# Earlier maxima of w1, q in long rows, and the tangent on one engine, in a fused attention and two-layer-pair kernel

## The chip, the cores and the metric

The kernel runs on one core of a Trainium2 chip. The metric is the device time of one launch in microseconds (us). Of the kernel before there are three timed runs and one profiled execution.

## The reference

What is computed, with the shapes that matter (B = 8 batches, H = 8 heads, S = 576 positions, D = 64; 4608 tokens, 512 model columns, 2048 hidden columns):

```python
kv = einsum('bhsd,bhse->bhde', k, v)
out = einsum('bhsd,bhde->bhse', q, kv)
rms = sqrt(mean(out * out, axis=-1, keepdims=True) + 1e-06)
x = (out / rms * g_norm)            # -> (4608, 512) tokens x columns
h = x @ moe_w_in                    # (512, 2048)
x = maximum(0.01 * h, h) @ moe_w_out    # (2048, 512)
h = x @ moe2_w_in
out = (h - tanh(h)) @ moe2_w_out
```

q, k, v and g_norm come as 32-bit floats, the four weights as 64-bit floats, which the kernel reads as pairs of 32-bit words.

## The kernel before, in words

The work has five stages. First comes a **start** of some 85 us: the attention of batch 0 and most of batch 1, and the making of the first weight matrix. Then come four **phases** of matrix products (one per weight matrix), in which TensorE works on the 16-bit halves of operands.

**Products.** Each phase multiplies by Strassen's method: of every 2x2 block of operands seven products are formed (the loop over `order` in `up`, the tables `PROD` and `BANK_OF`), and each product is three 16-bit matmuls per slice (high times high, high times low, low times high; line 513 in `three`). For that each operand is cut into seven forms: three blocks as they are and four sums. The names in the profile: `opa` holds the three plain forms of a left operand, `ops` the four sums, `w` the weights, `ps_a` to `ps_d` are the accumulators, `c` and `u` partial results kept by ScalarE, `g` the result, added up by VectorE (line 575).

**Weights.** `convert` turns one unit (of 16 per matrix) of 64-bit words into 32-bit floats: ScalarE takes the upper words' absolute values (line 329), VectorE clamps them and takes their maximum along (line 333), shifts, and puts in the lower words and the sign (lines 340, 346, 352). When all 16 units are through, `weight_scale` (lines 265 to 280) makes a scale from the greatest value: a reduction, a small transpose on TensorE (`pt`, line 234), two VectorE operations, a small matmul that spreads it (`pb`, line 244), then `s_w` and for w1 `s1g`. `right_stages` makes the forms of a unit: ScalarE writes the high halves (line 378) and VectorE the low ones (line 381), in two pieces of three and four blocks each, and the sums between (lines 388 and 392) are GpSimd's. The second and third matrix are converted while the first two phases run.

**Attention.** `load_pair` loads k, v and q of two heads (lines 812 and 818), k and v in rows of 1536 bytes, q in pieces of 256 bytes, so that both heads' columns lie side by side. `pair` gives TensorE the steps: `pk` (k times v, line 834, twelve small matmuls at two column positions), `pq` (q turned, line 854, two groups of three transposes of 96 by 128), `po` (line 870), and after every second pair `pm` (the means, line 907). ScalarE copies `kvd` and `qt` (lines 845, 862) and squares (line 876). `norms` takes the root and the reciprocal (lines 929, 937), stores them to HBM, loads them back broadcast as `bc` (lines 940, 946), and GpSimd multiplies `xg` by them (line 952). `left_stages` then makes `opa` and `ops` (lines 452 and 459; the four sums on GpSimd, line 491).

**The tangent.** In phase three `tanh` has ScalarE compute tanh of a whole 128x1024 tile (line 1246); VectorE subtracts one half of it and GpSimd the other (both line 1249).

**Order.** Every engine executes its queue in the order in which it was written. That order comes from a planner (class `Plan`): each step has an estimated duration, `fit` finds a free stretch on its engine, and what is due is issued in order of planned time. TensorE's own sequence is fixed by `on_pe`, at a planned time `plan.pe` that begins at `START`; in `between1` the attention steps of later batches are put between the products. If a step is planned before what it needs, the planner stops with an assertion.

Of the kernel before, what the change touches and what calls it, by code (L numbers as in the profile page):

```python
# [27 lines left out]
PROD = {1: (6, 5), 2: (4, 4), 3: (0, 6), 4: (5, 0), 5: (3, 1), 6: (1, 2), 7: (2, 3)}  # L28
BLOCKS = ("11", "21", "12", "22")
NOP = 7  # L30
# [18 lines left out]
class Plan:  # L49
# [7 lines left out]
    def __init__(self):  # L57
        self.heap, self.n, self.pe = [], 0, 0.0
        self.taken = {e: [] for e in "AVG"}

# [50 lines left out]
    def on_pe(self, dur, fn):  # L111

        self.at(self.pe, fn)
        self.pe += dur
        return self.pe

    def run(self):
        while self.heap:
            self.now, _, fn = heapq.heappop(self.heap)
            fn()  # L120


class Slots:


    def __init__(self, pool, kind, nbytes, n):
        self.pool, self.kind, self.nbytes = pool, kind, nbytes
        self.idle = list(range(n))
# [12 lines left out]
def body(ctx, tc, q, k, v, g_norm, w1, w2, w3, w4, out):  # L141
    nc = tc.nc
    B, H, S, D = q.shape
    NT, DM = out.shape
    DFF = w1.shape[1]
# [12 lines left out]
    const = ctx.enter_context(tc.tile_pool(name="const", bufs=1))  # L158
    wpool = ctx.enter_context(tc.tile_pool(name="wpool", bufs=1))
    work = ctx.enter_context(tc.tile_pool(name="work", bufs=1))  # L160
    dram = ctx.enter_context(tc.tile_pool(name="dram", bufs=1, space=DRAM))
    ps = ctx.enter_context(tc.tile_pool(name="ps", bufs=1, space=PSUM))
    L, M, X = Slots(work, "l", 16 * T1, NL), Slots(work, "m", 2 * 2 * NOP * P, NM), Slots(work, "x", 4 * T1, NX)
    plan = Plan()
# [4 lines left out]
    def bank(n, name):  # L169
        assert n not in used, (n, name)  # L170
        used.add(n)
        return ps.tile([P, 512], F32, tag=f"p{n}", name=name)

# [16 lines left out]

    def need(what):
        assert what in done_, ("planned too late", plan.now, what)
# [12 lines left out]
    sel = const.tile([P, 2 * Q - 2], F32, name="sel")  # L205
    kvd = [const.tile([P, P], F32, name=f"kvd{n}") for n in range(2)]

    def constants():
        for h in range(2):
            nc.sync.dma_start(out=gcol[D * h:D * h + D, :], in_=g_norm.rearrange("(p o) -> p o", o=1))  # L210
        make_identity(nc, ident)
# [3 lines left out]
        for n in range(2):  # L215
            nc.vector.memset(sel[D * n:D * n + D, Q - 2 + n:Q - 1 + n], 1.0 / D)
            nc.vector.memset(kvd[n], 0.0)
        nc.vector.tensor_reduce(out=gabs, in_=gcol, axis=AX.X, op=ALU.max, apply_absolute_value=True)
# [41 lines left out]
    def weight_scale(n, t):  # L260
# [16 lines left out]
        def last():  # L277
# [3 lines left out]
            done_.add(f"s_{name}")  # L281
# [25 lines left out]
    def convert(n, i, kk, t, land, keep=None):  # L307
# [42 lines left out]
        def high():  # L350
# [5 lines left out]
            converted[n] += 1  # L356
            if converted[n] == 2 * NP:
                weight_scale(n, plan.now + 1.0)

        def store():  # L360
            done_.add(("wf", n, i, kk))
            nc.sync.dma_start(out=wf[n, i, kk], in_=held["ap"])
            M.give(held["o"])

        slow = 1.0 if keep else 1.1
        steps = [(None, land, load), (None, 0.0, room), ("A", 0.7, one), ("V", 0.72 * slow, two), ("V", 0.4 * slow, shift),
                 ("V", 0.63 * slow, low), ("V", 0.63 * slow, high)]
        plan.chain(t, steps + ([(None, 0.0, store)] if keep is None else []))

    def right_stages(w, dst, scale, minus4, merged=False):  # L370
# [3 lines left out]
        def cols(n0, n1):  # L374
            return w().rearrange("p (o c) -> p o c", c=P)[:, n0:n1]

        def hi(a, b, n):
            nc.scalar.activation(out=dst()[:, 0, a:b], in_=cols(0, n), func=AF.Identity, scale=scale())  # L378

        def lo(a, b, n):  # L380
            nc.vector.scalar_tensor_tensor(  # L381
                out=dst()[:, 1, a:b], in0=cols(0, n), scalar=scale(), in1=dst()[:, 0, a:b],
                op0=ALU.mult, op1=ALU.subtract,
            )

        def both(e):
            b = w().rearrange("p (o c) -> p o c", c=P)
# [959 lines left out]
```

## Time and profile before

| | |
|---|---|
| Median of 3 runs | 1518.32 us (1515.48 to 1521.1) |
| Profiled execution: time, span | 1515.43 us, 1513.7 us |
| TensorE busy | 1440.1 us (95%) |
| VectorE busy | 1248.8 us (83%) |
| ScalarE busy | 914.5 us (60%) |
| GpSimd busy | 687.4 us (45%) |
| DMA | 323.17 MB in 188926 packets, 54112 of them under 512 B |

The span is the time from the first to the last instruction of the profiled execution; the 1.7 us between it and the time lie around it. PE is TensorE, PEld its weight loads, DVE VectorE, ACT ScalarE, POOL GpSimd, SP the engine that issues the DMAs. "PEclk" is the granted clock of TensorE as a share of full speed. A busy share is a mean over stages, and each stage is to be read by itself. In a timeline, the number in brackets is the idle time of the engine before the row, and behind it is what ended it; consecutive rows overlap at their edges, so the pace of a stream is the distance between starts.

### The profile page before, as it was taken

How to read it: one execution, taken by the hardware profiler on the slowest of the kernel's cores; microseconds unless marked ns; L12 is line 12 of the kernel's file. 1: busy time of each engine (PE TensorE's matmuls, PEld its weight loads, DVE VectorE, ACT ScalarE, POOL GpSimd, SP SyncE). 2: the span in 40 equal slices, each digit the busy share in tenths (PEclk: the TensorE clock that was granted, in tenths of full speed). 3: DMA queues.
4: the chain of work that ended last, by engine and by line, in shares of the span. 5: the costliest groups of instructions: out<-in, count | busy, mean ns of one | idle time of the engine just before them, and what ended most of it. 6: DMA issues, size and time to landing. Idle time of an engine off the chain costs nothing. (4 is left out here: it accounts for less than half of the span.)

```text
span 1513.7 us, 32951 instructions
## 1 busy us (share of the span) xinstructions
PE 1440.1 (95%) x12658; PEld 1192.3 (79%) x12658; DVE 1248.8 (83%) x2019; ACT 914.5 (60%) x1525; POOL 687.4 (45%) x646
## 2 busy tenths in 40 slices
PE   5299999999899999999999999999998999999998
PEld 3167777777677777777777888888887888888887
DVE  4885777787777899999997888978999988888871
ACT  5377777777667645445543677778887554445540
POOL 0474330452542455445442355558885643444430
PEclk8589999999999999999999999999999999999999
DMA  9829998999978845555645866546768644444431
GB/s 265 202 62 249 289 297 247 312 281 328 305 243 283 327 154 186 199 176 176 202 162 189 320 220 211 205 169 223 266 246 300 240 156 144 146 147 141 143 96 36
DMA packets 188926, 323.17 MB, mean 214 GB/s; under 512 B 54112, under 2 KB 130912, under 8 KB 188768
## 3 DMA queue, kind: packets, MB, share of 16 engines
q1 hardware_dynamic: 188768, 321.06, 65.9%
q8 instruction: 99, 1.62, 0.4%
q14 instruction: 59, 0.48, 0.1%
HBM read 190.84 MB, written 130.15 MB: 212 GB/s over the span
## 5 line engine op out<-in xcount | busy, mean ns | idle before, releaser
L513 PEld LDWEIGHTS <-w 128*128 128x128 f16 x8400 | 819.6, 98 | 204.0 <-issue 29.7
L491 POOL TENSOR_TENSOR gl<-gl 128x256 f32<-128x256 f32 (+1 forms) x272 | 297.0, 1094 | 368.9 <-DVE gl L491 142.2
L513 PE MATMUL ps_a<-ops,w 128*128 128x288 f16 (+1 forms) x2400 | 330.9, 282 | 6.7 <-ACT u L564 4.8
L513 PE MATMUL ps_c<-ops,w 128*128 128x288 f16 (+1 forms) x2352 | 315.3, 282 | 12.2 <-DVE g L575 12.2
L513 PE MATMUL ps_a<-opa,w 128*128 128x288 f16 (+1 forms) x2016 | 283.8, 281 | 0.2
L513 PEld LDWEIGHTS <-ops 128*128 128x128 f16 x1728 | 169.1, 98 | 21.6 <-issue 2.0
L513 PE MATMUL ps_b<-opa,w 128*128 128x288 f16 (+1 forms) x1200 | 175.5, 283 | 0.0
L491 DVE TENSOR_TENSOR gl<-gl 128x256 f32<-128x256 f32 (+1 forms) x272 | 151.5, 558 | 4.3
L1249 POOL TENSOR_TENSOR g<-g,th 128x512 f32<-128x512 f32 x72 | 113.3, 1574 | 82.1 <-ACT th L1246 68.8
L513 PEld LDWEIGHTS <-opa 128*128 128x128 f16 x1296 | 126.8, 98 | 14.7
L461 DVE SCALAR_TENSOR_TENSOR ops<-gl,inv,ops 128x1024 f16<-128x1024 f32 x72 | 102.9, 1429 | 29.4 <-ACT ops L454 29.3
L952 POOL TENSOR_TENSOR xg<-xg,bc 128x1152 f32<-128x1152 f32 x16 | 47.4, 2967 | 174.7 <-DMA bc<-iv 125.7
L454 ACT ACTIVATE ops<-gl,inv 128x1024 f16<-128x1024 f32 x72 | 82.4, 1144 | 62.9 <-POOL gl L491 62.9
L452 ACT ACTIVATE ops<-gl 128x1152 f16<-128x1152 f32 x64 | 74.3, 1161 | 74.8 <-POOL gl L491 72.8
L575 DVE SCALAR_TENSOR_TENSOR g<-ps_c,u 128x288 f32<-128x288 f32 x128 | 58.1, 454 | 50.3 <-PE ps_c L513 48.5
L459 DVE TENSOR_TENSOR ops<-gl,ops 128x1152 f16<-128x1152 f32 x64 | 93.5, 1461 | 4.8 <-ACT ops L452 4.7
L513 PE MATMUL ps_c<-w,ops 128*128 128x256 f16 x864 | 97.3, 273 | 0.2 <-DVE osb L575 0.2
L513 PE MATMUL ps_a<-w,ops 128*128 128x256 f16 x864 | 95.8, 273 | 1.4 <-ACT c L566 1.4
L566 ACT ACTIVATE u<-ps_a,up 128x256 f32<-128x256 f32 x144 | 68.1, 473 | 47.1 <-PE ps_a L513 43.4
L378 ACT ACTIVATE wo<-unit,s_w 128x384 f16<-128x384 f32 (+1 forms) x96 | 63.1, 662 | 52.3 <-DVE unit L392 45.5
L491 POOL TENSOR_TENSOR x1g<-x1g 128x256 f32<-128x256 f32 x72 | 65.3, 908 | 49.4 <-DVE opa L461 43.0
L381 DVE SCALAR_TENSOR_TENSOR wo<-unit,s_w,wo 128x384 f16<-128x384 f32 (+1 forms) x96 | 84.8, 891 | 1.6 <-ACT wo L378 1.4
(126 smaller groups left out, 2171.0 us busy)
## 6 DMA issues: line engine op xcount, KB each, us to landing
g<-g SPq DMA_DIRECT2D x64, 576.0 KB, 6.4
gl<-g SPq DMA_DIRECT2D x64, 576.0 KB, 4.7
g<-g SPq DMA_DIRECT2D x72, 512.0 KB, 3.3
gl<-g SPq DMA_DIRECT2D x72, 512.0 KB, 4.4
wd<-wo SPq DMA_DIRECT2D x48, 448.0 KB, 3.3
w<-wd SPq DMA_DIRECT2D x24, 896.0 KB, 7.4
words<-in_moe_w_in_dram SPq DMA_DIRECT2D x64, 256.0 KB, 6.2
words<-in_moe_w_out_dram SPq DMA_DIRECT2D x64, 256.0 KB, 4.8
```

Source lines behind the costliest of these rows:

```text
L378: nc.scalar.activation(out=dst()[:, 0, a:b], in_=cols(0, n), func=AF.Identity, scale=scale())
L381: nc.vector.scalar_tensor_tensor(out=dst()[:, 1, a:b], in0=cols(0, n), scalar=scale(), in1=dst()[:, 0, a:b], op0=ALU.mult, op1=ALU.subtract,)
L452: nc.scalar.activation(out=o, in_=i_, func=AF.Copy)
L454: nc.scalar.activation(out=o, in_=i_, func=AF.Identity, scale=scale())
L459: nc.vector.tensor_tensor(out=o, in0=i_, in1=h, op=ALU.subtract)
L461: nc.vector.scalar_tensor_tensor(out=o, in0=i_, scalar=scale(), in1=h, op0=ALU.mult, op1=ALU.subtract)
L491: lambda: e.tensor_tensor(out=g()[:, o], in0=g()[:, a], in1=g()[:, b], op=op),
L513: nc.tensor.matmul(out=out_, lhsT=a, rhs=c, start=start and m == 0, stop=stop and m == n - 1, skip_group_check=not fresh,)
L566: nc.scalar.activation(out=t, in_=src, func=AF.Identity, scale=self.scale)
L575: nc.vector.scalar_tensor_tensor(out=o, in0=src, scalar=self.minus if sub else self.scale, in1=t, op0=ALU.mult, op1=ALU.add,)
L952: e.tensor_tensor(out=x, in0=x, in1=held[kk].ap[:, n0:n1], op=ALU.mult)
L1249: e.tensor_tensor(out=g()[:, n], in0=g()[:, n], in1=held["t"].ap[:, n], op=ALU.subtract)
```

## The change

The start is arranged anew, the attention's q is loaded and turned in another way, the weights' forms are laid out and cut in another way, and phase three's subtraction moves to one engine. In detail:

- **w1.** Units of blocks 5, 6 and 7 (6 of 16) are not converted when they land: VectorE only takes the maximum of their upper words (`most`, line 465), and the rest of the conversion (`later`) comes after the scale. The first ten are converted as before. The loads of batch 1's pairs are put in front of and behind w1's last units, and three of these pairs' steps run directly after batch 0's.
- **Weights' forms.** The sums (`sums`, lines 496 and 500) come first, and high and low halves of all seven blocks are one instruction each (`parts`, lines 516 and 519; `PROD` numbers the blocks anew for that). For w1's first two blocks GpSimd forms the sums before the scale is known.
- **Batch 0's norm.** The reciprocal is one instruction, its broadcast goes through TensorE (`wide`, line 1096, eight matmuls with a selecting matrix `hot`) instead of HBM, and VectorE multiplies (line 1102) and forms the sums.
- **q.** One DMA of 1536-byte rows per pair instead of two of 256-byte pieces, in all batches. The heads are apart in it, so each group of three transposes becomes six plain matmuls against the identity, at column positions 0 and 64 (line 975).
- **The tangent.** VectorE subtracts both halves (line 1419), and GpSimd none.
- **The planner.** It first runs dry and notes, where a step would come before what it needs, by how much TensorE's planned time has to be put off; that moves the planned times, and no instruction waits by it. `SLOW` goes.

```diff
-            apart = nm != "q"
...
-            for h in range(2):
-                nc.sync.dma_start(out=held[nm].ap[:, :, h], in_=src[b, 2 * c + h].rearrange("(p c) d -> p c d", p=CP))
+            held[nm] = L.take([CP, 2, NC, D], F32, nm)
+            nc.sync.dma_start(
+                out=held[nm].ap.rearrange("p h c d -> p h (c d)"),
+                in_=src[b, 2 * c:2 * c + 2].rearrange("h (p c) d -> p h (c d)", p=CP),
+            )
...
-                nc.tensor.transpose(
-                    qt[r][0][:, CP * a:CP * a + CP], two_heads(held["q"], r * NC // 2 + a), ident[:CP, :CP]
-                )
+                for h in range(2):
+                    nc.tensor.matmul(
+                        out=qt[r][0][D * h:D * h + D, CP * a:CP * a + CP], lhsT=held["q"].ap[:, h, r * NC // 2 + a],
+                        rhs=ident[:CP, :CP], start=True, stop=True, tile_position=(0, D * h), skip_group_check=True,
+                    )
...
+        def most():
+            nc.vector.tensor_reduce(
+                out=mw[:, n, 2 * i + kk:2 * i + kk + 1], in_=held["w"].ap[:, 1::2].bitcast(F32), axis=AX.X, op=ALU.max,
+                apply_absolute_value=True,
+            )
+            count(n)
...
+        if later is not None:
+            plan.chain(t, [(None, land, load), ("V", 0.65, most)])
+            later.append([
+                (None, 0.0, room), ("A", 0.7, one), ("V", 0.42, clamp), ("V", 0.42, shift), ("V", 0.69, low), ("V", 0.69, high),
+            ])
+            return
...
+        def hi():
+            nc.scalar.activation(out=dst()[:, 0], in_=cols(), func=AF.Identity, scale=scale())
+
+        def lo():
+            nc.vector.scalar_tensor_tensor(
+                out=dst()[:, 1], in0=cols(), scalar=scale(), in1=dst()[:, 0], op0=ALU.mult, op1=ALU.subtract,
+            )
+
+        return [("A", 1.15, hi), ("V", 1.25, lo)]
...
+            nc.tensor.matmul(
+                out=held["b", kk, n][:, :T1], lhsT=hot["t"].ap[:, kk, n], rhs=held["iv"], start=True, stop=True,
+            )
...
+            nc.vector.tensor_tensor(out=x, in0=x, in1=held["b", kk, n][:, :T1], op=ALU.mult)
...
-        order += [("w",) + u for u in UNITS[hp:hp + 1]]
-    order += [("w",) + u for u in UNITS[4:]]
+        order += [("w",) + u for u in UNITS[2 * hp:2 * hp + 2]]
+    order += [("w",) + u for u in UNITS[8:14]] + [("a", 1, PAIRS[0])] + [("w",) + u for u in UNITS[14:]]
+    order += [("a", 1, PAIRS[hp]) for hp in range(1, 4)]
...
-    START = last + 45.0
+    last = ta[1, PAIRS[0]][0]
+    for hp in range(EARLY):
+        early_pair(1, PAIRS[hp], last + 0.8, ta[1, PAIRS[hp]][1])
+        last += 6.0
+    START = last + GAP
...
-            [("V", 0.65, lambda: two(nc.vector, slice(0, 2))), ("G", 1.5, lambda: two(nc.gpsimd, slice(2, 4)))],
+            ("V", 0.62, lambda: two(0)), ("V", 0.62, lambda: two(1)),
```

Three places show how the queues move. The first is VectorE's queue in the start, around w1's scale (`m_w` is the greatest value, `opa` the attention's operand, `mw` the units' maxima, `xg` the attention's result). Before:

```order
L352 SCALAR_TENSOR_TENSOR w1f_643<-words,w1f_643 128x512 x2
L459 TENSOR_TENSOR opa<-xg,opa 128x288
L265 TENSOR_REDUCE m_w_690<-mw 128x1
L267 TENSOR_SCALAR t_w_691<-m_w_690 128x1
L270 SCALAR_TENSOR_TENSOR m_w_690<-m_w_690,t_w_691 128x1
```

After:

```order
L465 TENSOR_REDUCE mw<-words 128x1
L1007 COPY xg<-po 128x288
L360 TENSOR_REDUCE m_w_750<-mw 128x1
L362 TENSOR_SCALAR t_w_751<-m_w_750 128x1
L365 SCALAR_TENSOR_TENSOR m_w_750<-m_w_750,t_w_751 128x1
```

The row ahead of `m_w` was batch 0's operand; now it is a copy of batch 1's first attention result.

The second is TensorE's queue from the spreading of the scale to the first product (`ps_a<-opa`). Before:

```order
L244 MATMUL pb<-diag_w_708,ones 128x1
L854 MATMUL pq<-ident,q 128x96 x6
L870 MATMUL po<-qt,kvd_325 128x288 x2
L834 MATMUL pk<-v,k 64x64 x12
L854 MATMUL pq<-ident,q 128x96 x6
L870 MATMUL po<-qt,kvd_326 128x288 x2
L907 MATMUL pm<-sq,sel 32x288 x4
L834 MATMUL pk<-v,k 64x64 x12
L854 MATMUL pq<-ident,q 128x96 x6
L870 MATMUL po<-qt,kvd_325 128x288 x2
L513 LDWEIGHTS w_0_746
```

After:

```order
L339 MATMUL pb<-diag_w_765,ones 128x1
L975 MATMUL pq<-ident,q 64x96 x12
L992 MATMUL po<-qt,kvd_328 128x288 x2
L1029 MATMUL pm<-sq,sel 32x288 x4
L954 MATMUL pk<-v,k 64x64 x12
L975 MATMUL pq<-ident,q 64x96 x12
L992 MATMUL po<-qt,kvd_327 128x288 x2
L637 LDWEIGHTS w_0_814
```

One pair fewer stands behind the scale, since the first of batch 1 now runs ahead of it, and the rows of q are twice as many and half as wide.

The third is VectorE's queue late in phase three (`th` is the tanh, `gl` and `opa` and `ops` are operands of phase four). Before:

```order
L575 SCALAR_TENSOR_TENSOR g<-ps_c,up_11119,u_15784 128x256
L491 TENSOR_TENSOR gl<-gl 128x256
L575 SCALAR_TENSOR_TENSOR g<-ps_c,up_11119,u_15667 128x256
L461 SCALAR_TENSOR_TENSOR opa<-gl,inv_10539,opa 128x768
L1249 TENSOR_TENSOR g<-g,th 128x512
L575 SCALAR_TENSOR_TENSOR g<-ps_b,up_11119,c_15772 128x256
L491 TENSOR_TENSOR gl<-gl 128x256
L461 SCALAR_TENSOR_TENSOR ops<-gl,inv_10539,ops 128x1024
```

After:

```order
L705 SCALAR_TENSOR_TENSOR g<-ps_c,up_11208,u_15761 128x256
L614 TENSOR_TENSOR gl<-gl 128x256
L705 SCALAR_TENSOR_TENSOR g<-ps_c,up_11208,u_15644 128x256
L1419 TENSOR_TENSOR g<-g,th 128x512
L583 SCALAR_TENSOR_TENSOR ops<-gl,inv_10628,ops 128x1024
L705 SCALAR_TENSOR_TENSOR g<-ps_b,up_11208,c_15751 128x256
L1419 TENSOR_TENSOR g<-g,th 128x512
L583 SCALAR_TENSOR_TENSOR opa<-gl,inv_10628,opa 128x768
```

Each result's tanh now takes two rows of VectorE's queue instead of one, and they need not stand together.

## Rows read from the trace of the kernel before

**Rows 1.** Windows by stage: us, busy us per engine (count), clock, DMA share, GB/s.

```profile
0.00:84.69 84.69, 38.14 (x266) 22.77 (x267) 57.30 (x122) 37.29 (x80) 26.80 (x29) 0.69 0.86 209
84.69:480.00 395.31, 383.58 (x3464) 295.18 (x3463) 296.60 (x552) 285.42 (x575) 156.42 (x162) 0.99 0.87 266
...
860.00:1194.00 334.00, 326.43 (x2963) 290.47 (x2962) 302.28 (x477) 256.25 (x431) 216.52 (x195) 0.99 0.67 238
```

**Rows 2.** Timeline of TensorE, first 100 us: start, us, what [idle before].

```profile
64.91 0.37 PE L234 MATMUL pt<-ident,m_w 128*1 128x128 f32 x1 [29.18 <-DVE m_w L274]
65.21 1.55 PE L834 MATMUL pk<-v,k 96*64 96x64 f32 x24
...
74.95 2.19 PE L870 MATMUL po<-qt,kvd 128*128 128x288 f32 x4
77.07 1.74 PE L907 MATMUL pm<-sq,sel 128*32 128x288 f32 x8
...
84.69 1.65 PE L513 MATMUL ps_a<-opa,w 128*128 128x288 f16 x6
...
87.61 0.90 PE L513 MATMUL ps_a<-ops,w 128*128 128x288 f16 x6
```

**Rows 3.** Timeline of VectorE, first 100 us.

```profile
62.30 1.90 DVE L459 TENSOR_TENSOR opa<-xg,opa 128x288 f16<-128x288 f32 x1 [3.46 <-ACT opa L452]
64.12 0.16 DVE L265 TENSOR_REDUCE m_w<-mw 128x1 f32<-128x16 f32 x1
...
68.44 0.75 DVE L280 TENSOR_TENSOR s1g<-s_w,gcol 128x1 f32<-128x1 f32 x1
...
81.28 0.75 DVE L381 SCALAR_TENSOR_TENSOR w<-w1f,s1g,w 128x512 f16<-128x512 f32 x1 [0.17 <-ACT w L378]
...
86.49 0.46 DVE L885 COPY xg<-po 128x288 f32<-128x288 f32 x1 [1.40 <-ACT sq L876]
```

**Rows 4.** Timeline of ScalarE, first 100 us: the last conversion of w1.

```profile
45.15 0.66 ACT L329 ACTIVATE w1f<-words 128x512 f32<-128x512 f32 x1 [0.76 <-DMA words<-in_moe_w_in_dram]
```

**Rows 5.** Windows of 10 us at the start, same columns.

```profile
20.00:30.00 10.00, 6.39 (x69) 3.75 (x63) 3.81 (x8) 5.15 (x13) 0.00 (x0) 0.98 1.13 298
30.00:40.00 10.00, 4.45 (x15) 1.81 (x15) 9.84 (x26) 8.51 (x17) 0.00 (x0) 0.50 1.09 348
```

**Rows 6.** Timeline of TensorE in the first product phase.

```profile
203.41 0.41 PE L854 MATMUL pq<-ident,q 96*128 96x96 f32 x3
203.66 0.90 PE L513 MATMUL ps_a<-ops,w 128*128 128x288 f16 x6
...
210.51 0.90 PE L513 MATMUL ps_a<-opa,w 128*128 128x288 f16 x6
211.34 0.92 PE L834 MATMUL pk<-v,k 96*64 96x64 f32 x24
212.19 0.91 PE L513 MATMUL ps_c<-ops,w 128*128 128x288 f16 x6
```

**Rows 7.** Waits of TensorE from 84.69 to 480 us: total, times, longest.

```profile
PE ps_a L513 <- ACT u L564: 4.8, 2, 4.1
PE ps_c L513 <- DVE g L575: 4.8, 7, 1.3
```

**Rows 8.** Timeline of TensorE around the longest of these waits.

```profile
392.24 1.60 PE L513 MATMUL ps_a<-ops,w 128*128 128x288 f16 x6 [4.13 <-ACT u L564]
...
398.70 0.90 PE L513 MATMUL ps_a<-opa,w 128*128 128x288 f16 x6
```

**Rows 9.** Waits of TensorE from 860 to 1194 us.

```profile
PE ps_c L513 <- DVE g L575: 6.6, 5, 3.1
```

**Rows 10.** Groups by form, VectorE, 860 to 1194 us: busy us, mean ns.

```profile
L1249 DVE TENSOR_TENSOR g<-g,th 128x512 f32<-128x512 f32 x70 | 65.8, 940 | 4.1 <-ACT th L1246 3.9
```

**Rows 11.** The same on GpSimd.

```profile
L1249 POOL TENSOR_TENSOR g<-g,th 128x512 f32<-128x512 f32 x69 | 108.9, 1579 | 76.8 <-ACT th L1246 63.5 <-DMA words<-in_moe_w_out_dram 6.8 <-DMA x1g<-x 6.0
```

**Rows 12.** All instructions of line 1249 on VectorE: duration ns min/median/max.

```profile
L1249 DVE TENSOR_TENSOR g<-g,th x72: 673/693/1768, 851.5 to 1183.4; 128x512 f32<-128x512 f32 x72
```

More of the change, by code (lines that the diff above doesn't have):

```diff
@@ L111, in on_pe, with go, miss, met @@
     def on_pe(self, dur, fn):
-        self.at(self.pe, fn)
+        k = self.ops
+        self.ops += 1
+        self.pe += self.delays.get(k, 0.0)
+        def go():
+            self.op = k
+            fn()
+            self.op = None
+        self.at(self.pe, go)
         self.pe += dur
         return self.pe
+    def miss(self, key):
+        if not self.dry or self.op is None and self.first is None:
+            raise AssertionError(("planned too late", self.now, key))
+        if self.first is None:
+            self.first = self.op, key, self.now
+        raise Missed
+    def met(self, key):
+        if self.first and self.first[1] == key:
+            raise Resolved
     def run(self):
@@ L189, in body, with done @@
     done_ = set()
+    def done(*what):
+        for x in what:
+            done_.add(x)
+            plan.met(x)
     def need(what):
-        assert what in done_, ("planned too late", plan.now, what)
+        if what not in done_:
+            plan.miss(what)
     def when(what, t, fn):
@@ L368, in convert @@
[L368 to L383, printed above, removed]
-            )
+        def most():
[3 more added lines that the diff above has]
+            )
+            count(n)
@@ L440, in load_weights, with left_stages @@
         )
-    def left_stages(g, dst, scale, T, done=None, first=None, pieces=1, rest=None, gps=None):
+    def left_stages(g, dst, scale, T, over=None, first=None, pieces=1, rest=None, gps=None):
         f = T / 1000.0
@@ L502, in part @@
         kind = "A" if a >= 4 else "S"
-        assert kind in ops.get("ready", ""), ("planned too late", plan.now, kind)
+        if kind not in ops.get("ready", ""):
+            plan.miss(("part", id(ops), kind))
         return ops["A"].ap[:, h, a - 4] if a >= 4 else ops["S"].ap[:, h, a]
@@ L546, in bank @@
             need = {6: "c1", 7: "u2", 3: "22", 4: "u3" if self.one4 else None}.get(p)
-            assert need is None or need in self.done, ("planned too late", plan.now, need)
+            if need is not None and need not in self.done:
+                plan.miss((id(self), need))
             start = p in (1, 2, 5) or p == 4 and not self.one4
@@ L1096, in body @@
     end1 = plan.pe
+    T0 = marks[50]
     def spread(fn, units, t0, t1):
```

328 lines of the change are left out of this document (208 added, 120 removed).

## The prediction

> **What bounds the kernel now.** I read the windows by stage first [rows 1]. The reader is to see that TensorE is busy for 383.6 of 395.3 us in the first product phase and for 326.4 of 334 in the third, but for 38 of 84.7 us in the start, at a mean clock of 0.69. So behind 84.69 us time is gained or lost only as TensorE's queue gets shorter or longer, or as one of its few waits goes; the start is where it idles.
>
> Next the timelines of the start. TensorE waits 29 us for `m_w` [rows 2], the greatest value of w1. The last words of w1 are taken up at 45.15 us [rows 4], but `m_w` is reduced at 64.12 us, because an attention operand stands ahead of it in VectorE's queue, and that waited for ScalarE's half of it [rows 3]. The scale `s1g` follows at about 69 us, the first product at 84.69, the first product with the four sums at 87.61 [rows 2, 3]. Last the waits of the product phases: 11.7 us of idle time in phase one, of which the two largest kinds make 9.6 [rows 1, 7], and 6.6 us late in phase three, all for VectorE's additions [rows 9].
>
> **The start.** Ahead of `m_w` now stand the last unit's maximum and a copy of batch 1's first attention result, so whichever is later counts.
>
> *Words.* One more pair (three tiles of 96x768 floats, 0.88 MB) is loaded ahead of the last two units: 2.5 us at 348 GB/s. Against that the q pieces of 256 bytes go: 298 GB/s moved with them, 348 without [rows 5], so batch 0's 3.5 MB and the words between them come some 3 to 4 us sooner. The last maximum is due at 43 to 45 us.
>
> *The copy.* The reciprocal stands behind the maximum of the fourteenth unit. By then 10.9 of 12.8 MB have come, at about 37 us, so I take 40 us for its end. Behind it TensorE runs five of the broadcasts, one `pk`, two groups of q and one `po`. A 128x288 matmul in 32 bits takes 1.06 us at the lower clock level (1.2 GHz): four records, two matmuls, 74.95 to 77.07 us [rows 2]. `pk` takes 1.5 there, a group of q I set at 1.2. That is 5 x 1.06 + 1.5 + 2.4 + 1.06 = 10.3 us, or about 5 at the upper level (2.4 GHz). A square and the copy itself add 0.9. So `m_w` begins at 46 to 51 us, later than the words allow; I take 48.
>
> *The scale.* From `m_w` to `s1g` were 5 us [rows 3], with foreign work between the steps as now, so `s1g` is due at 53 us.
>
> *First product.* Behind the spreading of the scale TensorE still has four groups of q, four `po`, a `pm` and a `pk`: 4 x 1.2 + 4 x 1.06 + 1.7 + 1.5 = 12.2 us at the lower level, 6 at the upper. With 9 the first product comes at 62 us, 23 us sooner than before.
>
> *First product with the sums.* It needs the sums of both halves, which VectorE now forms itself. Behind its last copy stand, ahead of the last piece of `ops`, five low halves of weights (128x896; 0.75 us for 512 columns [rows 3], so I take 1.1), four pieces of `ops` (0.7 each) and five small operations (0.4 to 0.46, as the copy [rows 3]): 5.5 + 2.8 + 2 = 10.3 us. Between the two products lay 2.9 us; now 10. So it starts at 72 us instead of 87.6. TensorE idles some 6 us of these 10, and after a wait of 4.13 us before it ran at the lower level from 392.24 to 398.70 us [rows 8], which lost 3.2 us. Net gain of the start: 15.6 - 3.2 = 12 us. Its bounds are 5 us (all at the lower level: `s1g` at 57, the first product at 69, the sums at 79) and 20 us (all at the upper level, the additions between them unhindered). The weights that follow are no limit: VectorE needs some 20 us for the remaining nine low halves and six late units, while TensorE works over 40 us on the first eight blocks.
>
> **q in plain matmuls.** In phase one a group of three transposes takes 0.25 us of TensorE's stream (203.41 to 203.66 [rows 6]). Its three records become twelve: six matmuls of two records each, as `pk` shows 24 records for twelve matmuls. `pk` has the same two column positions and 64 moving columns; it takes 0.85 us, and 0.09 us pass ahead of it beyond the 0.74 us that six records of the product take [rows 6]. A group has half its matmuls and 96 columns: 0.85 x 6/12 x 96/64 = 0.64 us, and the 0.09: 0.73, so 0.48 more than before. If the part of `pk` that does not scale with columns is fixed for a matmul, it is 0.42 more; I take 0.45. After the start 25 pairs remain, so 50 groups: +22 us, all of it on TensorE's queue in the phase that TensorE bounds. Bounds: 0.23 more where both column positions overlap fully (0.48 us for three times 96 columns at the pace of `po`, half of 1.06 us for 288) makes +11.5; no overlap (0.96 us, with the gaps 1.27) makes +51. The row nearest to it is `pk`, and it overlaps.
>
> The Trainium skill, "TensorEngine Tiling", under Restrictions and Gotchas, says that column tiling excludes the transpose mode for 32-bit input, so the turned q has to be a plain matmul here; "TensorE: Matmul & The Clock Gate", in its Terms, gives that mode as four times faster for FP32. By that a group would cost 1.0 us without and 0.5 with overlap, +37 or +12 us in all; no row here shows the new form, and `pk` lies between the two.
>
> **What that gives back.** Phase one loses 11.7 us of idle time and the 3.2 us at the lower level. The longest wait was for ScalarE; the others for VectorE. TensorE now takes 22 us longer for the same rows of these engines, and the DMA queue, busy at 0.87 on the mean [rows 1], loses q's small pieces. I let 9 of the 15 us go; bounds 0 and 15, since the order of the weights' stores behind the longest wait is planned anew.
>
> **The tangent.** GpSimd's half took 1579 ns [rows 11], VectorE's 940 on the mean, 673 at least [rows 10, 12]. Two halves without GpSimd beside them cost VectorE about 1.3 us for 0.94 per tile, +0.4 x 70 = +25 us on 302 of 334 [rows 1]. What it gives back: GpSimd loses 108.9 of its 216.5 us, and it is beside GpSimd's work that VectorE's half stretched from 673 to as much as 1768 ns. If half of that stretching (0.27 us on the mean) goes from all of some 300 operations on SBUF that VectorE does here, it is 20 to 40 us, so VectorE's load hardly changes. TensorE feels it only where VectorE is late, in the 6.6 us of five waits [rows 9] and the clock behind the last. I take -3 us; bounds -9 (all waits go) and +7 (no relief, 20 results x 0.33 us where VectorE is full).
>
> The Trainium skill, "SBUF — State Buffer", under SBUF: two separate sides, has GpSimd and a VectorE operation with two SBUF inputs lock each other out of a shared port for a whole instruction. The spread from 673 to 1768 ns agrees with it. By that rule alone the waits of phase three would all go, which is the -9.
>
> Merging two pieces of weights into one instruction saves a little VectorE time in phases two and three, where products hide it: nothing. The planner's dry run issues nothing.
>
> **Sum.** -12 (start) + 22 (q) - 9 (waits of phase one) - 3 (phase three) = -2 us. From the profiled time of 1515.43 us that is 1513.4. The profiled execution lies 2.9 us under the median of the runs shown, 1518.3, so the median after is due at 1516 us.
>
> **Rivals.**
> *Cheap q, warm start.* Both column positions overlap fully (+11.5 us) and TensorE reaches the upper level while it waits for the copy (-18). Then with the same -12 of waits the result is -18, about 1500 us; halfway to it 1508. For it: the broadcasts are dense matmuls, and the level had risen by 20 to 30 us in the start [rows 5]. Against it: it stayed low in the whole stretch of attention from 65 to 85 us [rows 2], and `pk` does not overlap fully.
> *Dear q, late sums.* The q groups cost 0.5 us or more each and the sums come at 79 us: +26 - 5 - 7 - 1 = +13, 1531 us; without any overlap +51 instead of +26, 1556. It is slower from the point at which q's groups cost more than the start and the waits give back, about 0.6 us each with the sums at 75 us. For it: the phase it lengthens has hardly any slack. Against it: `pk` [rows 6].
> *VectorE becomes the bound of phase three.* No relief from GpSimd, +25 us on 302 of 334 leaves 7 us of slack; TensorE's waits double: +7 instead of -3, that is 1526 us. For it: these waits were VectorE's already. Against it: the spread of line 1249.
>
> **How the numbers follow.** The forecast, within 0.5% (7.6 us, about what a measurement of this kernel can tell from no change), 0.40, its own range 1511 to 1526; the cheap-q case 0.34, faster by more; the dear-q case 0.18 and VectorE's 0.08, slower by more. The range, 1500 to 1531, takes in both sides' main points and leaves out full serial q and a start at its best bound.
>
> **What would show it.** Right: the first product at 58 to 66 us and the first with `ops` 8 to 11 us later; q's groups at 0.65 to 0.75 us of stream; phase one longer by some 13 us from its first sums to its end; line 1419 near 0.68 us. Wrong: `m_w` right behind the last words, at 45 us; q's groups at 0.5 us or at over 1; idle time of TensorE in phase one above 12 us; waits for line 705 in phase three above 7 us.

## The result and the profile after

The changed kernel took 1528.23 us (median of 11 runs, 1523.9 to 1532.81); the kernel before, in 11 runs on the same chips, 1520.48. The ratio is 1.006, with an interval from 1.0045 to 1.0076. So the change costs some 7 to 12 us; the forecast was a gain of 2 us, within what cannot be told from no change. The profiled execution took 1525.99 us with a span of 1524.2.

To see where the time went, I took TensorE's 11424 product matmuls in order and asked when the one starts with which each share of them is reached. The table gives that time for the kernel before, and how much later (+) or earlier (-) the others are there, each from its one profiled execution; the columns behind "changed" are experiments told below. Phase one ends at 0.235 of the products, phase two at 0.47, phase three at 0.735. The profiled execution of before lies 5 us under its median now and the others lie up to 4 us on either side of theirs, so the columns are to be compared with each other, stretch by stretch, and their ends read a few microseconds too high.

```
share   before  changed  q_before    nl22  split22  small22  small22_b2c  b_rows
0.010    104.1     -7.7      -8.4    -6.1     -2.6     -5.4         -6.0    +1.0
0.040    161.0     -4.8     -10.1    -3.3     +0.2     -7.0         -7.6    +4.6
0.060    199.6     +0.2      -3.7    -0.5     +6.1     +0.1         -3.8    +6.8
0.125    315.0    +10.0      -1.1    +8.8    +15.1     +3.7         -1.2   +15.8
0.225    488.3     +7.5      -2.4    +7.5    +14.4     +4.3         -0.8   +15.3
0.500    873.8     +7.8      -1.6    +7.6    +15.1     +4.4         -0.5   +16.6
0.700   1123.8     +8.1      -0.7    +7.9    +16.9     +4.7         -0.2   +16.6
0.850   1321.9    +10.5      +1.6    +4.7    +18.4     +2.3         -3.7   +17.6
```

Read down the changed kernel's column: the start gains 7.7 us, phase one loses 15.2, phase two changes nothing to speak of, and the stretch from phase three into phase four (0.5 to 0.85) loses 2.7. The forecast had -12, +13 and -3.

The start. Timeline of TensorE in the changed kernel, columns as in [rows 2]:

```profile
45.19 1.33 PE L1096 MATMUL pb<-iv,hot 128*128 128x288 f32 x2 [10.08 <-DVE iv L1059]
...
68.36 0.65 PE L637 MATMUL ps_a<-opa,w 128*128 128x288 f16 x4
...
72.18 0.28 PE L637 MATMUL ps_a<-ops,w 128*128 128x288 f16 x1 [0.89 <-ACT ops L574]
74.64 0.92 PE L637 MATMUL ps_a<-ops,w 128*128 128x288 f16 x3 [2.18 <-DVE ops L581]
78.11 0.64 PE L637 MATMUL ps_a<-ops,w 128*128 128x288 f16 x2 [2.54 <-DVE ops L581]
...
82.00 0.91 PE L637 MATMUL ps_a<-ops,w 128*128 128x288 f16 x6
```

And of VectorE, for [rows 3]:

```profile
42.59 0.69 DVE L465 TENSOR_REDUCE mw<-words 128x1 f32<-128x512 f32 x1 [0.29 <-DMA words<-in_moe_w_in_dram]
43.19 1.94 DVE L1059 RECIPROCAL iv<-iv 128x288 f32<-128x288 f32 x1
...
50.30 0.69 DVE L465 TENSOR_REDUCE mw<-words 128x1 f32<-128x512 f32 x1 [0.51 <-DMA words<-in_moe_w_in_dram]
55.53 0.46 DVE L1007 COPY xg<-po 128x288 f32<-128x288 f32 x1 [4.54 <-ACT sq L998]
55.90 0.16 DVE L360 TENSOR_REDUCE m_w<-mw 128x1 f32<-128x16 f32 x1
...
62.01 0.15 DVE L375 TENSOR_TENSOR s1g<-s_w,gcol 128x1 f32<-128x1 f32 x1
...
79.37 0.75 DVE L581 TENSOR_TENSOR ops<-xg,ops 128x576 f16<-128x576 f32 x1
```

The first product starts at 68.36 us (before: 84.69), the first that runs through with the four sums at 82.00 (before: 87.61); three short pieces stand between, each waiting for a piece of `ops`.

Phase one. Windows as in [rows 1], then the waits of TensorE as in [rows 7], then a group of q and a `po` among the products as in [rows 6]:

```profile
68.36:487.60 419.24, 407.75 (x3915) 303.61 (x3913) 309.88 (x560) 293.49 (x558) 146.15 (x144) 0.99 0.80 251
```

```profile
PE ps_a L637 <- DVE ops L581: 4.7, 2, 2.5
PE ps_c L637 <- DVE g L705: 4.6, 7, 2.3
PE pk L954 <- DMA v<-in_v_dram: 1.0, 1, 1.0
PE ps_a L637 <- ACT ops L574: 0.9, 1, 0.9
```

```profile
203.35 0.90 PE L637 MATMUL ps_b<-opa,w 128*128 128x288 f16 x6
204.18 0.72 PE L975 MATMUL pq<-ident,q 96*64 96x96 f32 x12
204.82 0.91 PE L637 MATMUL ps_a<-ops,w 128*128 128x288 f16 x6
205.57 0.90 PE L637 MATMUL ps_a<-opa,w 128*128 128x288 f16 x6
206.30 0.65 PE L992 MATMUL po<-qt,kvd 128*128 128x288 f32 x2
206.79 0.90 PE L637 MATMUL ps_c<-ops,w 128*128 128x288 f16 x6
```

In the kernel before, the products ahead of the group of [rows 6]:

```profile
202.67 0.90 PE L513 MATMUL ps_b<-opa,w 128*128 128x288 f16 x6
```

A group of q takes 0.64 us of the stream (204.18 to 204.82; 0.25 before). The six product records ahead of it take 0.83 us (203.35 to 204.18), where the kernel before has 0.74 (202.67 to 203.41), so another 0.09 us belongs to the group: 0.73 us, 0.48 more than before. The 50 groups from the first product on make +24 us. The idle time behind the start's 5.6 us is down to 5.9 us, and DMA is busy at 0.80 instead of 0.87.

Phase three. The waits of TensorE from 867.4 to 1202 us, for [rows 9]; VectorE's group by form, for [rows 10]:

```profile
PE ps_a L637 <- ACT u L696: 5.7, 1, 5.7
PE ps_c L637 <- DVE g L705: 2.2, 3, 1.5
```

```profile
L1419 DVE TENSOR_TENSOR g<-g,th 128x512 f32<-128x512 f32 x141 | 108.9, 782 | 3.6 <-ACT th L1415 3.6
```

VectorE's half takes 782 ns on the mean instead of 940, and the waits for its additions fall from 6.6 to 2.2 us, but a wait for ScalarE of 5.7 us is new. Here is how it comes about: VectorE, SyncE (the store's issue), ScalarE and TensorE in turn, one timeline each:

```profile
1177.07 2.31 DVE L1419 TENSOR_TENSOR g<-g,th 128x512 f32<-128x512 f32 x2
```

```profile
1179.41 0.32 SPq L784 DMA_DIRECT2D g<-g  x1
```

```profile
1174.52 0.48 ACT L696 ACTIVATE g<-ps_a,up 128x256 f32<-128x256 f32 x1
1182.94 1.06 ACT L1415 ACTIVATE th<-g 128x1024 f32<-128x1024 f32 x1 [7.93 <-DMA g<-g]
1183.90 0.46 ACT L696 ACTIVATE u<-ps_a,up 128x256 f32<-128x256 f32 x1
```

```profile
1184.41 1.44 PE L637 MATMUL ps_a<-opa,w 128*128 128x256 f16 x6 [5.73 <-ACT u L696]
```

VectorE ends a subtraction at 1179.38; its result is stored from 1179.41. The next tangent wants a large buffer, gets the one that this store is still reading, and so begins at 1182.94 after 7.93 us. ScalarE works in order, so the reading of a product bank that TensorE needs (line 696) stands behind it.

### The profile page after: what moved, and what is told of

Read it like the earlier page. It is cut to its first block, busy times and chain, and to the rows that moved or that the text cites. A ratio compares the mean times of both kernels' runs of the same rounds, so it can differ in the third digit from the quotient of the medians.

```text
span 1524.2 us, 33929 instructions
## 1 busy us (share of the span) xinstructions
PE 1469.2 (96%) x13250; PEld 1207.1 (79%) x13250; DVE 1259.3 (83%) x2043; ACT 907.9 (60%) x1461; POOL 572.7 (38%) x564
## 5 line engine op out<-in xcount | busy, mean ns | idle before, releaser
L614 POOL TENSOR_TENSOR gl<-gl 128x256 f32<-128x256 f32 (+1 forms) x272 | 307.0, 1130 | 397.1 <-DVE gl L614 174.2
L614 POOL TENSOR_TENSOR x1g<-x1g 128x256 f32<-128x256 f32 x72 | 68.4, 953 | 171.8 <-DVE opa L583 150.9
L1419 DVE TENSOR_TENSOR g<-g,th 128x512 f32<-128x512 f32 x144 | 110.9, 780 | 3.6 <-ACT th L1415 3.6
L1074 POOL TENSOR_TENSOR xg<-xg,bc 128x1152 f32<-128x1152 f32 x14 | 39.5, 2821 | 148.0 <-DMA bc<-iv 104.9
L1415 ACT ACTIVATE th<-g 128x1024 f32<-128x1024 f32 x72 | 75.5, 1048 | 15.3 <-DMA g<-g 13.2
L581 DVE TENSOR_TENSOR opa<-gl,opa 128x864 f16<-128x864 f32 x64 | 79.8, 1247 | 3.7 <-ACT opa L574 3.3
```

The source lines that it names most:

```text
L581: nc.vector.tensor_tensor(out=o, in0=i_, in1=h, op=ALU.subtract)
L614: lambda: e.tensor_tensor(out=g()[:, o], in0=g()[:, a], in1=g()[:, b], op=op),
L1074: e.tensor_tensor(out=x, in0=x, in1=held[kk].ap[:, n0:n1], op=ALU.mult)
L1415: nc.scalar.activation(out=held["t"].ap, in_=g(), func=AF.Tanh)
L1419: nc.vector.tensor_tensor(out=o, in0=o, in1=held["t"].ap[:, 2 * n:2 * n + 2], op=ALU.subtract)
```

## Experiments

Each ran in five rounds beside the kernel before. A ratio is to that kernel's own runs (medians 1518.4 to 1519.1 us).

### The price of q

**q_twice** issues each group of q's matmuls two times from batch 1 on.

```diff
-                for h in range(2):
+                for h in (0, 1) if b == 0 else (0, 1, 0, 1):
```

> The changed kernel with every group of q's plain matmuls issued twice from batch 1 on (56 groups, six of them in the start); the second writes what the first wrote. Theory A (all of a group's 0.65 us is TensorE's): 50 groups in phase one, +32 us, less at most the 6 us of idle time that is left there: 1554 to 1560 us. Rival B (q's matmuls run in time that TensorE would lose anyway, and phase one is longer for another reason): +10 us or less, under 1540 us.

1550.93 us, ratio 1.0209 [1.0192, 1.0226]: 22.7 us above the changed kernel, under theory A's 26 and far over rival B's 10. The reason for the miss stands in TensorE's timeline:

```profile
244.85 1.21 PE L975 MATMUL pq<-ident,q 96*64 96x96 f32 x24
245.99 0.91 PE L637 MATMUL ps_c<-ops,w 128*128 128x288 f16 x6
```

The doubled group takes 1.14 us of stream, not 1.28. So twelve records cost 0.50 us, and what is left of the 0.73, 0.14 us behind the group and 0.09 ahead of it, comes once; 50 x 0.50 = 25 us, and the idle time shrank by 3. All of it is on TensorE's queue.

**q_before** turns q as before, with pieces of 256 bytes and transposes, in all batches; **q_rows_start** does so from batch 2 on (`b <= 1` in place of `False`).

```diff
-            held[nm] = L.take([CP, 2, NC, D], F32, nm)
+            apart = nm != "q" or False
+            held[nm] = L.take([CP, 2, NC, D] if apart else [CP, NC, 2, D], F32, nm)
...
+                if not (False):
+                    nc.tensor.transpose(
```

> The changed kernel, but from batch 2 on q comes in pieces of 256 bytes and is turned by transposes as before; only batches 0 and 1 keep the long rows and the plain matmuls. Theory A (the plain matmuls stand on TensorE's queue): 48 groups go from 0.65 us of stream back to 0.25, 19 us; the changed kernel had some 6 us less idle time in phase one than the one before, which comes back, so 13 us net: a median of about 1515 us, ratio to the kernel before 0.997, and a lag behind the kernel before that stays at -6 to -8 us through phase one. Rival B (the new places of the attention pairs and the planner's waits cost the time, not q's form): no change, about 1528 us, and a lag that grows to +6 us over phase one as it did. Rival C (small pieces of q slow the loads): as A in TensorE's stream, but waits for DMA above 5 us and about 1522 us.

> The changed kernel with q loaded in pieces of 256 bytes and turned by transposes in all batches, the start included. Theory A (long rows bring the words of w1 3 to 4 us sooner, as the prediction has it, and little else in the start): the first product comes 2 to 4 us later than 68.4 and the time is 1 to 4 us above the version that keeps long rows in batches 0 and 1 (1519.5): 1520 to 1524 us. Rival B (the plain matmuls of q, at the lower clock level in the start, cost as much there as the long rows bring): within 1.5 us of 1519.5, or below it.

They took 1519.54 us (1.0008 [0.9993, 1.0024]) and 1519.32 us (1.0007 [0.9995, 1.0019]): the same. So q's form costs the changed kernel 8.9 us net, less than theory A's 13, and long rows in the start are worth nothing to the time: with small pieces `m_w` comes at 54.48 us here, 55.90 in the changed kernel. Less than 13, because phase one, freed of 24 us of stream, waits elsewhere: TensorE is idle for 22.6 of the 411.4 us from 68.60 to 480, for 11.5 in the changed kernel's window. In q_before TensorE's waits from 100 to 480 us are:

```profile
PE ps_c L637 <- DVE g L705: 8.6, 8, 2.7
PE pk L959 <- DMA v<-in_v_dram: 4.6, 2, 4.1
PE ps_a L637 <- ACT u L694: 3.1, 1, 3.1
```

The wait for `v` is a DMA's, as rival C had it, and a little under the 5 us that it asked for (1.0 in the changed kernel).

**b_rows** is the kernel before with long rows and plain matmuls for q, and nothing else.

```diff
-            apart = nm != "q"
+            apart = True
...
-                nc.tensor.transpose(
-                    qt[r][0][:, CP * a:CP * a + CP], two_heads(held["q"], r * NC // 2 + a), ident[:CP, :CP]
-                )
+                for h in range(2):
+                    nc.tensor.matmul(
```

> The kernel before, with q alone in long rows and turned by the plain matmuls, in all batches, and nothing else changed. Theory A (the prediction's terms for q: 22 us on TensorE's queue, of which the idle time of phase one and the lighter loads give 9 to 12 back): 8 to 13 us above the kernel before, 1526 to 1531 us, with 3 to 6 us of idle time left in phase one. Rival B (the loads gain as much as TensorE loses): within 3 us of the kernel before.

1530.55 us, 1.0083 [1.0066, 1.0099]: 11 to 13 us above the kernel before, theory A. Its first product comes at 84.47 us (before 84.69): the long rows bring nothing to that start either. Its phase one, windows as in [rows 1]:

```profile
84.70:490.00 405.30, 398.24 (x3869) 297.39 (x3867) 293.23 (x546) 287.35 (x569) 152.87 (x160) 1.00 0.80 255
```

The idle time is 7.1 us for 11.7, and the clock is 1.00 throughout, where the kernel before ran some 10 us of its phase one at the lower level (0.99 on the mean).

**q_pairs** keeps the long rows and turns q by transposes after all.

```diff
-        def qtr(r):
+        def qtr(h):
+            qt["p", h] = att_bank("pq")
+            for j in range(NC // 2):
+                nc.tensor.transpose(
+                    qt["p", h][0][:, CP * j:CP * j + CP],
+                    held["q"].ap[:, h, 2 * j:2 * j + 2].rearrange("p c d -> p (c d)"), ident[:CP, :CP],
+                )
...
+                    nc.scalar.activation(
+                        out=qt[r].ap[D * h:D * h + D], in_=src[D * r:D * r + D, :T1], func=AF.Copy
+                    )
...
+            c = 2 * (c % 3) + c // 3
```

> The changed kernel with q in long rows, but turned by transposes: a transpose takes two neighbouring token groups of one head (128 words that lie together), so a group of q is three transposes again; ScalarE then copies each half of the partitions to where it belongs (four copies of 64x288 for a pair instead of two of 128x288), and the tokens of a batch go through the kernel in another order, undone as the output is stored. Theory A (TensorE's stream for the plain matmuls and the small pieces on the DMA queue are two separate prices, and this pays neither): groups at 0.25 us, 20 us less on TensorE; no DMA-caused waits above those of the changed kernel (1 us), idle time in phase one 6 to 12 us: 1510 to 1517 us, under the 1519.5 of the version with small pieces. Rival B (phase one is bound by ScalarE and VectorE once TensorE's stream is short, whatever the loads do): idle time near 19 us as with the small pieces, 1518 to 1523 us.

1533.99 us, 1.0098 [1.0082, 1.0114]: neither. TensorE's longest waits from 100 to 480 us show what came in between:

```profile
PE ps_a L637 <- ACT u L694: 9.8, 4, 5.7
PE ps_c L637 <- DVE g L705: 8.6, 5, 2.9
PE ps_a L637 <- DVE w L519: 7.1, 2, 5.9
```

The doubled copies take ScalarE 402 ns for half of the partitions, as much as the whole did (410). The last weights of w1 moved in the queues, and their low halves fell beside GpSimd's scaling of a batch (107.82 to 114.22 us), where an operation of VectorE that takes 0.68 us elsewhere took 3.11 (line 452 at 108.64 us); TensorE waited 7.1 us for them. That the copies alone cause this is not shown, and whether another order saves this form stays open.

### The start

**late_off** converts all units of w1 as they land.

```diff
-    LATE, EARLY, GAP = (5, 6, 7), 3, 0.0
+    LATE, EARLY, GAP = (), 3, 0.0
```

> The changed kernel without the late maxima: all units of w1 are converted as they come, ahead of the scale. Theory A (the late maxima bring the scale forward): the maximum over all units comes some 12 to 18 us later than the 55.9 us of the changed kernel, the first product of phase one at 78 to 86 us instead of 68.4, and some of it is given back since no conversions stand among the first weights; the time is 4 to 12 us longer, 1532 to 1540 us. Rival B (the broadcasts on TensorE and the sums on VectorE make the gain, and the first product with the sums is bound by VectorE's work in any order): within 3 us of 1528.

1537.11 us, 1.012 [1.0101, 1.0139]: 8.9 us longer, theory A. `m_w` comes at 77.18 us, 21 us later (theory A had 12 to 18), the first product at 84.17. The late maxima do what they say, and some of their gain is given back behind the first product.

**copy_act** lets ScalarE copy the early results of batch 1.

```diff
-                if b == 0:
+                if b == 0 or b == 1 and c in PAIRS[:EARLY]:
```

> The changed kernel with the attention results of batch 1 that are made in the start copied by ScalarE instead of VectorE, so that no copy stands ahead of the greatest value of w1. Theory A (the start was 4 us worse than forecast because that value waited for a copy behind TensorE's queue): the value is reduced at 51 to 52 us instead of 55.9, the first product with all of the sums comes 3 to 6 us sooner than 82.0, and the time falls by 2 to 5 us, to 1523 to 1526 us. Rival B (VectorE's additions and low halves, without a gap from 61 us on, set the sums, and the spreading of the scale stands behind TensorE's queue anyway): the value comes sooner but the sums by less than 2 us, and the time is within 2 us of 1528.

1531.2 us, 1.0076 [1.0064, 1.0089]: 3 us slower, though `m_w` comes at 52.61 us and the first full product with the sums at 78.06, 4 us sooner. So neither theory holds: the sums come sooner, as A has it, and the time does not fall. By the count of the table it leads the kernel before by 9.9 us at 0.01 of the products (the changed kernel by 7.7), and by 1.3 at 0.04 (4.8). In between TensorE is idle for 4.8 us (100 to 170 us; the changed kernel not at all), 1.9 of it for weights, in these two rows, the rest for additions and copies:

```profile
115.89 0.42 PE L637 MATMUL ps_a<-opa,w 128*128 128x288 f16 x2 [1.13 <-ACT w L516]
117.12 0.30 PE L637 MATMUL ps_a<-opa,w 128*128 128x288 f16 x1 [0.81 <-DVE w L519]
```

### The tangent

**tanh_split** gives GpSimd its half back.

```diff
-            ("V", 0.62, lambda: two(0)), ("V", 0.62, lambda: two(1)),
+            [("V", 0.65, lambda: two(0)), ("G", 1.5, lambda: two(1))],
```

> The changed kernel with the tangent taken off by VectorE and GpSimd in halves again. Theory A (GpSimd's half and the stretching that it causes cost VectorE as much as the second half does, and the end of phase three is set by ScalarE's wait for a buffer): VectorE's busy time in phase three stays within 10 us of the 306 it has now, its half has a mean near 0.9 us again, and the time changes by less than 4 us: 1524 to 1532 us. Rival B (VectorE alone is what lengthens phase three): 4 to 8 us faster, 1520 to 1524 us, with no wait for line 696 there.

1524.75 us, 1.0047 [1.0034, 1.0061], 3.5 us below the changed kernel. The wait for line 696 is down to 1.1 us, and the waits for VectorE's additions are back at 7.6. Which theory holds can't be read from this run: its time lies in A's range and 0.8 us outside B's. From 0.5 to 0.85 of the products it still loses 2.2 us on the kernel before (7.1 to 9.3), with the tangent done as there; so something else in the change (the weights' merged pieces, the planner's order) may cost that much in this stretch, and I did not separate it.

**nl22** has one large buffer more, **split22** that and the halves of tanh_split.

```diff
-    NL, NM, NX = 21, 12, 8
+    NL, NM, NX = 22, 11, 8
```

> The changed kernel with 22 large buffers instead of 21 (and 11 instead of 12 of the middle kind). Theory A (late in phase three the tangent's buffer is the one that a stored result has just left, so ScalarE waits for that store, and TensorE for ScalarE, 5.7 us at 1178 us): with one buffer more the buffer taken there is an older one, the wait for line 696 shrinks below 2 us and the time falls by 3 to 5 us, to 1523 to 1525 us. Rival B (the buffer is not what ends the wait: ScalarE's tangent is late because VectorE's queue is full): a wait of over 4 us stays there for line 696 or 705, and the time is within 2 us of 1528.

> The changed kernel with 22 large buffers (11 of the middle kind) and the tangent taken off by VectorE and GpSimd in halves, as before. Beside the 1523.3 us of the same kernel with VectorE alone this prices the tangent's step by itself, without the wait for the buffer. Theory A (GpSimd's half stretches VectorE, which is late at the end of phase three; VectorE alone is late less): the waits for line 705 late in phase three are 6 to 8 us instead of 4, and the time is 2 to 4 us above 1523.3: 1525 to 1527 us. Rival B (the step is worth nothing; the buffer did it all): within 1 us of 1523.3.

nl22 took 1523.25 us, 1.0031 [1.0019, 1.0042], 5.0 us below the changed kernel: theory A. TensorE's waits from 860 to 1300 us in nl22, and in split22:

```profile
PE ps_c L637 <- DVE g L705: 4.2, 4, 2.0
PE ps_a L637 <- ACT u L696: 0.8, 1, 0.8
```

```profile
PE ps_c L637 <- DVE g L705: 7.4, 5, 3.0
PE ps_a L637 <- ACT c L696: 2.5, 2, 2.1
PE ps_a L637 <- ACT u L696: 1.1, 1, 1.1
```

split22 took 1530.08 us, 1.0074 [1.0056, 1.0092], 6.8 us above nl22 and more than theory A had. From 0.5 to 0.85 of the products nl22 gains 2.9 us on the kernel before, split22 loses 3.3; that difference of 6.2 is the tangent's. With the buffer out of the way VectorE alone is the better form by about 6 us; with it in the way, it is 0.6 us (the same stretch) to 3.5 us (the medians) worse. The stretch can be trusted, since it repeats: the changed kernel and the six experiments that share its tangent and its 21 buffers lose 2.6 to 3.3 us there, the three with 22 (nl22 and the two of the next section) gain some 2 to 3, and nl22 issues the changed kernel's instructions of TensorE, VectorE and GpSimd in the same order, so that little but the buffers differs. split22 was also behind nl22 at 0.01 to 0.225 of the products, where the two kernels issue the same instructions (the last section).

### Both losses undone

**small22** is q_before with 22 large buffers; **small22_b2c** moreover puts the attention of batch 2 earlier.

```diff
-    FIRST = {1: (None,) * EARLY + (0, 8, 16, 24)[:4 - EARLY], 2: (14, 25, 36, 47), 3: (60, 72, 84, 96)}
+    FIRST = {1: (None,) * EARLY + (0, 8, 16, 24)[:4 - EARLY], 2: (12, 22, 32, 42), 3: (60, 72, 84, 96)}
```

> The changed kernel with q as before (pieces of 256 bytes, transposes) in all batches and 22 large buffers instead of 21 (11 instead of 12 of the middle kind). Theory A (q's form and the tangent's buffer are two separate losses of the change): the sum of the two single steps, 1519.3 - 4.9 = 1514.4 us, a ratio to the kernel before near 0.997, with the start at -8 us against the kernel before, a wait for VectorE and ScalarE near 166 us that takes 6 us of it, and no wait over 2.5 us late in phase three. Rival B (with q's short stream phase one is tight elsewhere, and another count of buffers moves waits about): over 1517 us.

> As the one before, and the attention pairs of batch 2 stand 2 to 5 products earlier (at 12, 22, 32 and 42 instead of 14, 25, 36 and 47), so that its sums start earlier. Theory A (the start's gain of 8 us is given back where the operands of batch 2 are late: GpSimd waits for the broadcast of its scale, ScalarE for GpSimd, TensorE for ScalarE): the wait near 166 us goes and the time falls by another 4 to 8 us, to 1507 to 1511 us. Rival B (attention put earlier only pushes the products back, and the wait comes at another batch): within 2 us of the one before, with idle time of TensorE in phase one as large.

small22 took 1513.87 us, 0.9973 [0.9962, 0.9983], half a microsecond from the sum of the single steps; small22_b2c 1510.81 us, 0.9947 [0.993, 0.9964]. Both beat both kernels. The timelines show what the earlier places do. TensorE in small22, then in small22_b2c:

```profile
170.46 1.32 PE L637 MATMUL ps_a<-ops,w 128*128 128x288 f16 x6 [4.45 <-ACT u L694]
174.31 1.60 PE L637 MATMUL ps_c<-ops,w 128*128 128x288 f16 x6 [2.05 <-DVE g L705]
```

```profile
161.40 0.75 PE L1003 MATMUL po<-qt,kvd 128*128 128x288 f32 x2 [3.65 <-ACT qt L995]
```

GpSimd's second scaling of batch 2, in small22 and in small22_b2c:

```profile
166.54 2.61 POOL L1085 TENSOR_TENSOR xg<-xg,bc 128x1152 f32<-128x1152 f32 x1 [8.77 <-DMA bc<-iv]
```

```profile
157.48 2.61 POOL L1085 TENSOR_TENSOR xg<-xg,bc 128x1152 f32<-128x1152 f32 x1 [2.20 <-DMA bc<-iv]
```

GpSimd waits 8.77 us for the broadcast scale, ScalarE's high halves for GpSimd (7.98 us), TensorE for ScalarE and then VectorE (4.45 and 2.05), and the next products run at 1.32 and 1.60 us instead of 0.90. Put earlier, one wait of 3.65 us is left, for a copy of q that stands behind those high halves in ScalarE's queue; two products behind it run slow as well (1.28 and 1.60 us), but there is no second wait. The gain, 3.1 us by the medians and 4 by the ratios, is just under theory A's 4 to 8, though the time lies in its range.

## Why the prediction was wrong

**The start: forecast -12, measured -7.7** (in four other executions of the same start -7.3, -6.5, -6.1 and -2.6: q_rows_start, tanh_split, nl22, split22). The step that failed is "so I take 40 us for its end": the reciprocal ended at 45.13 us. It stands in VectorE's queue behind maxima that wait for words of w1, and the words land later than I set: the last maximum began at 50.30 us, not at 43 to 45. "Against that the q pieces of 256 bytes go", 3 to 4 us sooner, stays open: with small pieces the last maximum began at 51.47 us in q_before, between the 50.37 and 52.27 of copy_act and q_pairs, which have long rows, but at 55.67 and 56.46 in small22 and small22_b2c, against 52.63 in split22. The first product moved by less than 2 us either way: 68.64 us in q_before and 67.98 in q_pairs; 71.64 and 70.48 in small22 and small22_b2c and 72.02 in split22; 84.47 in b_rows and 84.69 before.

What follows the reciprocal was right in its terms: from TensorE's first broadcast (45.19) to the copy (55.53) are 10.3 us, as forecast for the lower clock level (I took 48 us for `m_w`, between the levels), from `m_w` to `s1g` 6.1 for 5, and from there to the first product 6.4, as forecast for the upper level (granted clock 1.00 from 60 to 70 us), where I took 9. Between the first product and the one with all the sums lay 13.6 us for 10. copy_act adds that an earlier `m_w` would not have been kept; "The weights that follow are no limit" is off there by 1.9 us of waits.

**q: forecast +22, measured 50 x 0.48 = +24 us of stream.** Right: 0.73 us a group, as scaled from `pk`. The parts are others, so that the sum fits is in some part luck: I scaled `pk` as a whole, but q_twice shows twelve records at 0.50 us, the pace of full overlap that the rival "cheap q" had, and 0.23 us that come once with each group. The Trainium skill's factor of four for transposes ("TensorE: Matmul & The Clock Gate", Terms) does not come out, and I had misapplied it: four times the 0.25 us of three transposes is 1.0 us for an overlapped group, not 0.5. The records' 0.50 us is twice the transposes' time.

**What that gives back: forecast -9.** Right in size: in b_rows, whose start is as before, 4.7 us of idle time and about 4.8 us of the lower level (half of some 10 us) go, 24 less these is 14.5, and its phase one is 14.3 us longer. In the changed kernel it is 15.2 where 13 were forecast. What I left out is that phase one gives part of the start back. Behind dear q that hardly shows (15.2 against 14.3); with q as before (q_before) phase one loses 6.0 us, all of it between 0.04 and 0.06, where batch 2's operands are late for products that come 8 to 10 us sooner. small22_b2c shows that about half of this can be mended.

**The tangent: forecast -3, measured +2.7 from 0.5 to 0.85 of the products.** The step that failed is "TensorE feels it only where VectorE is late". The relief was real: VectorE's half fell from 940 to 782 ns, its busy time in phase three stayed (302.3 and 304.3 us; 295.5 in tanh_split, so the step by itself adds 9), and the waits for its additions fell from 6.6 to 2.2 us. But ScalarE's next tangent needs a buffer, and I asked only which engine would be late, not which buffer. With one more, the same stretch gains 2.9 us, near the forecast. The Trainium skill's shared port ("SBUF — State Buffer", under SBUF: two separate sides) agrees with the shorter half; its result here, all waits gone, does not come out, since 2.2 us stay and another wait stood behind.

**The sum.** -7.7 + 15.2 + 0.3 (phase two) + 2.7 = +10.5 us in the profiled executions (7.8 by the medians), where the forecast had -2. Of the 12.5 us between, the stretch of phases three and four makes 5.7 (2.2 of it also with the tangent halved as before), the start 4.3, phase one 2.2, phase two 0.3. The rival "dear q, late sums" is nearest to the time, with its sums at 79 us (82.0 measured), but its q, +26, was hardly dearer than mine.

## What to carry to other kernels

A gain ahead of a phase can be lost in it again if that phase's own supplies do not move with it: look for the operand that was just in time before, and move it too. When work moves from one engine to another, follow the buffer as well as the engines: whose store or read must end before the buffer of the next step is free. And lighter loads paid for with matmuls (here 24 us of TensorE's stream) are a bad bargain in a phase that TensorE bounds.

## What the runs showed that I had not expected

- The same start ran at different clocks. nl22 and split22, on two chips, issue the same instructions up to phase three; TensorE's granted clock from 60 to 70 us was 1.00 (2.4 GHz) in the one and 0.66 on the mean in the other, part of it at the lower level, and split22 was 3.5 us later at 0.01 of the products. Windows of nl22, then of split22:

```profile
60.00:70.00 10.00, 9.71 (x133) 6.41 (x134) 8.62 (x22) 7.89 (x17) 0.00 (x0) 1.00 0.49 135
```

```profile
60.00:70.00 10.00, 9.75 (x100) 6.76 (x100) 6.51 (x18) 4.95 (x11) 0.00 (x0) 0.66 0.42 107
```

- A copy by ScalarE of 64 partitions by 288 words takes 402 ns, of 128 partitions 410.
- A group of q's plain matmuls costs TensorE 0.23 us beside its records, 0.09 ahead of it and 0.14 behind. It is not the change between 32 and 16 bits: `po`, plain matmuls in 32 bits too, costs nothing beside its records (0.73 us for the six product records ahead of it, 205.57 to 206.30 in the changed kernel, and 0.49 for its own two), nor do the transposes. `pk`, whose records are 96*64 like q's, has the 0.09 as well (210.51 to 211.34 in [rows 6]). So the narrower records go with the price; why, no run shows.
- q's records take 0.50 us for three times 96 columns at both column positions, as one 128x128 matmul in 32 bits over 288 columns does (`po`, 0.49 us, 206.30 to 206.79): by these numbers the two positions overlap fully.
